# Pooled attention and routed experts on one core: weights in the buffers of k, q and v, row writes held until the last v is in

## The chip, the cores and the metric

The kernel runs on one core of one Trainium2 chip. The metric is device time in microseconds (us) of one execution; where a median is given, it is over several runs. Engines are named as in the profile: PE is TensorE (matrix multiply), PEld its weight loads, DVE is VectorE, ACT is ScalarE, POOL is GpSimd, SP is the sync engine, which here only issues transfers.

## What is computed

Attention with pooled keys and values, and then one of eight experts for each token:

```python
k_p = k.reshape(B, H, Sp, 8, D).mean(axis=3)          # B, H, S, D = 8, 8, 576, 64
v_p = v.reshape(B, H, Sp, 8, D).mean(axis=3)
attn = softmax(q @ k_p.T / sqrt(D))
x = (attn @ v_p).transpose(0, 2, 1, 3).reshape(4608, 512)
for e in range(8):                                     # domain_id: the expert of each token
    mask = domain_id == e
    h = maximum(x[mask] @ w1[e], 0.0)                  # w1: (8, 512, 1024)
    out[mask] = h @ w2[e]                              # w2: (8, 1024, 512)
```

All inputs but domain_id are float32 in HBM; the kernel converts to float16 on the way in.

## The kernel before

**Stages.** Two batch entries are a *pair*; there are four pairs. For each pair, k, q and v (1152 KB each in float16) are loaded whole, one transfer each (load_pair, L107), on GpSimd's queue, which converts. k is pooled by matmuls and turned (kp_units, L416), q is turned (qt_units, L483), v is pooled and turned (vp_units, L449: nine units of matmuls evacuated in three operations at L467, then two folds evacuated at L479; all five evacuations on ScalarE). sc_unit (L499) makes scores and takes their exponential on ScalarE. av_unit (L512) multiplies by v, divides by the sum on VectorE (L530, L532) and leaves three chunks of 128 rows of x in an x_sb tile; after every third chunk SP writes that tile to x_lin in HBM (L541). There are twelve such writes, of 384 KB, three for each pair, and four x_sb tiles.

**Routing.** While attention runs, the kernel works out for each expert the list of its rows in x_lin (perm_units with two GpSimd operations a pair at L370, perm_mm, perm_finish) and of its output rows (orig_finish). An expert has room for 640 rows, five blocks of 128. gather (L583) brings one block from x_lin by an indirect transfer; turn_units (L590) turns blocks for use as the moving operand; l1_units (L623) multiply by w1 and apply the maximum, alternating between ScalarE (L638) and VectorE (L640); l2_units (L644) multiply by w2, evacuate y and scatter each block to the output by an indirect transfer of GpSimd (L659). The first 384 rows of experts 0 and 1 are filled from pairs 0 to 2 alone, so that they can start early: their gathers read only the first part of x_lin and need the first nine row writes.

**Order of the work.** The order is written out by hand. Every engine executes its instructions in program order. In attention, units are put into a plan with a due number (16 for each pair) and sorted by it (L678 to L743): loads, kp, vp, qt, av units, the routing, gathers and the first experts' units each have a due number, and nothing checks it against time. After that, lists of units are run one after the other (L753 to L784). pace (L606) makes GpSimd copy one element of the hidden tile before a gather, so that the gather isn't issued before a given L1 unit is done. An instruction with an unmet wait holds up what follows on its engine; this is true for GpSimd, which issues all loads, gathers and scatters, and for SP, which issues the row writes.

**Buffers.** k, q and v have two tiles of 9216 bytes per partition each. Weights (8192 bytes per partition, w1 and w2 of an expert) have four tiles of their own, tag "w", for experts 0, 1, 5 and 6; the other experts use tiles of k, q and v (W_AT, L559). PSUM tiles are big (two), wide (one) and small (two); rot2 takes big, big, wide in turn for scores, av and L1, and rot1 small, small, wide for L2, each by a counter that runs through the whole kernel.

**Rows of w1.** w1 is loaded so that partition p holds rows 4p to 4p+3, one stretch of 16 KB in HBM (L573). av_unit therefore writes the columns of x in a permuted order (L532). w2 is loaded with partition p holding rows 128k+p (L575).

## Time and profile before

| | us |
|---|---|
| median of 14 runs (261.87 to 265.96) | 264.09 |
| the profiled execution, its own time | 262.69 |
| its span | 261.0 |
| PE busy | 228.7 (88%) |
| DVE busy | 121.0 (46%) |
| POOL busy | 115.5 (44%) |
| ACT busy | 94.2 (36%) |
| software queue of DMA (loads, gathers, scatters) | 79.8% of 16 engines' span |
| hardware queue of DMA (row writes) | 5.0% of 16 engines' span |

The page divides the span into 40 slices of about 6.5 us and gives the busy share of each engine in tenths, the clock granted to TensorE (PEclk, tenths of full speed) and the mean busy share of the 16 DMA engines. In a timeline, a line is a run of equal instructions: start, time, engine, line of the kernel, operation, output and input tile; a bracket at its end gives the engine's idle time before it and what released it. A busy DMA engine or TensorE says where the work is, and the brackets say which wait ended last.

### The profile page before, as it was taken

To read this page: it belongs to the slowest core of one execution; us is meant where nothing else is said; L and a number is where in the kernel's file an instruction comes from. 1 tells how busy PE (TensorE), PEld (TensorE's weight loads), DVE (VectorE), ACT (ScalarE), POOL (GpSimd) and SP (SyncE) were. 2 spreads that over 40 slices of the span, in tenths; PEclk is the share of its full clock that TensorE was granted. 3 is DMA by queue.
4 is the path that set the end of the run, shared out by engine and by line. 5 is a ranking of instruction groups with operands and counts; after the bars stand their busy time and mean duration, and the time that the engine had idled before them with its cause. 6 is when DMAs were issued, how large, how long until landed. Compare 5 with 4: busy or idle time off the path is not lost.

```text
span 261.0 us, 5042 instructions
## 1 busy us (share of the span) xinstructions
PE 228.7 (88%) x2048; PEld 147.3 (56%) x2048; DVE 121.0 (46%) x275; ACT 94.2 (36%) x158; POOL 115.5 (44%) x157
## 2 busy tenths in 40 slices
PE   0788889999788679997966999999999999999991
PEld 0566566676466456555833655755745755756640
DVE  7356698786568444244421333333333332343320
ACT  1046767779367724232310321311311312302210
POOL 8001521300000670177870777676766676654043
PEclk9997999999989757999997999999999999999998
DMA  6999999999998299987899798989979978952022
GB/s 109 205 224 212 219 217 234 244 242 243 244 239 256 65 173 260 238 221 130 244 151 252 130 203 161 221 210 181 228 228 158 225 207 181 219 218 100 3 96 100
DMA packets 18298, 50.20 MB, mean 192 GB/s; under 512 B 2332, under 2 KB 10590, under 8 KB 15840
## 3 DMA queue, kind: packets, MB, share of 16 engines
q0 software_dynamic: 16464, 45.10, 79.8%
q1 hardware_dynamic: 1808, 4.76, 5.0%
q8 instruction: 16, 0.26, 0.4%
q14 instruction: 10, 0.08, 0.1%
HBM read 67.15 MB, written 15.20 MB: 315 GB/s over the span
## 4 chain that ended last, share of the span: by engine, by line
PE 54%; DMA 22%; issue 10%; POOL 6%; ACT 3%; DVE 2%; POOLq 1%
PE big L634 16%; PE small L650 13%; DMA q<-in_q_dram 12%; PE wide L634 7%; DMA v<-in_v_dram 7%; PE wide L650 6%; DMA xg<-x_lin,xrow 3%; POOL out_dram L659 3%; PE turn L598 3%; PE small L464 2%; PE big L506 2%; ACT at L509 1%; PE big L526 1%; PE wide L526 1%; PE small L492 1%
## 5 line engine op out<-in xcount | busy, mean ns | idle before, releaser
L584 POOL DMA_INDIRECT xg<-x_lin,xrow x40 | 41.6, 1040 | 50.1 <-DMA x_lin<-x_sb 36.3
L659 POOL DMA_INDIRECT out_dram<-y,tok x40 | 40.2, 1006 | 51.4 <-DVE y L655 27.8
L650 PEld LDWEIGHTS <-hT 128*128 128x128 f16 x272 | 26.3, 99 | 27.6 <-issue 1.7
L509 ACT ACTIVATE at<-big 72x576 f16<-72x576 f32 x45 | 28.7, 645 | 12.8 <-PE big L506 11.9
L634 PEld LDWEIGHTS <-w 128*128 128x128 f16 x256 | 25.3, 100 | 14.0 <-issue 4.9
L634 PE MATMUL big<-xT,w 128*128 128x320 f16 (+2 forms) x176 | 28.8, 311 | 1.4 <-DVE xT L599 1.4
L640 DVE TENSOR_SCALAR hT<-big 128x640 f16<-128x640 f32 (+1 forms) x21 | 15.3, 729 | 27.3 <-PE big L634 17.6
L657 ACT ACTIVATE y<-small 128x512 f32<-128x512 f32 x14 | 8.4, 597 | 49.8 <-PE small L650 38.2
L599 DVE COPY xT<-turn 128x1024 f16<-128x1024 f16 (+1 forms) x24 | 14.3, 597 | 23.1 <-PE turn L598 21.6
L638 ACT ACTIVATE hT<-big 128x640 f16<-128x640 f32 (+1 forms) x21 | 13.2, 628 | 25.8 <-PE big L634 23.9
L655 DVE COPY y<-small 128x512 f32<-128x512 f32 x13 | 9.0, 691 | 22.1 <-PE small L650 20.1
L650 PE MATMUL small<-w,hT 128*128 128x512 f16 x72 | 18.5, 403 | 0.0
L598 PE MATMUL turn<-ident,xg 128*128 128x128 f16 x160 | 14.1, 228 | 4.8 <-DMA xg<-x_lin,xrow 4.4
L526 PEld LDWEIGHTS <-at 72*128 72x128 f16 (+1 forms) x320 | 14.5, 108 | 6.5 <-issue 3.1
L598 PEld LDWEIGHTS <-xg 128*128 128x128 f16 x160 | 11.3, 102 | 11.2 <-DMA xg<-x_lin,xrow 4.6
L506 PE MATMUL big<-qT,kpT 64*72 64x288 f16 x90 | 14.9, 329 | 2.8 <-DVE qT L496 1.0
L634 PEld LDWEIGHTS <-k 128*128 128x128 f16 x128 | 12.5, 98 | 5.2
L634 PE MATMUL wide<-xT,w 128*128 128x320 f16 (+2 forms) x80 | 13.8, 306 | 1.4 <-DVE y L655 1.4
L532 DVE TENSOR_TENSOR x_sb<-big,rcp 128x512 f16<-128x512 f32 x21 | 14.5, 691 | 0.7
L492 PE MATMUL small<-ident,q 128*128 128x128 f16 x144 | 11.7, 231 | 3.4 <-DMA q<-in_q_dram 1.7
L640 DVE TENSOR_SCALAR hT<-wide 128x640 f16<-128x640 f32 (+1 forms) x11 | 7.9, 715 | 13.8 <-PE wide L634 11.8
L509 ACT ACTIVATE at<-wide 72x576 f16<-72x576 f32 x19 | 12.3, 646 | 5.5 <-PE wide L506 5.3
(155 smaller groups left out, 358.6 us busy)
## 6 DMA issues: line engine op xcount, KB each, us to landing
w<-in_moe_w_dram POOLq DMA_DIRECT2D x8, 1024.0 KB
k<-in_k_dram POOLq DMA_DIRECT2D x4, 1152.0 KB
v<-in_v_dram POOLq DMA_DIRECT2D x4, 1152.0 KB
x_lin<-x_sb SPq DMA_DIRECT2D x12, 384.0 KB, 10.7
q<-in_q_dram POOLq DMA_DIRECT2D x3, 1152.0 KB
k<-in_moe_w_dram POOLq DMA_DIRECT2D x3, 1024.0 KB
v<-in_moe_w_dram POOLq DMA_DIRECT2D x3, 1024.0 KB
q<-in_moe_w_dram POOLq DMA_DIRECT2D x2, 1024.0 KB
```

Source lines behind the costliest of these rows:

```text
L492: nc.tensor.transpose(p[:, j, :], qq[:, 128 * (j0 + j):128 * (j0 + j) + 128], ident[:])
L506: nc.tensor.matmul(p[0:72, par, 0:288], s["kpT"][64 * par:64 * par + 64, bh, :], s["qT"][64 * par:64 * par + 64, :, 8 * bh:8 * bh + 8], st ...
L509: nc.scalar.activation(at[0:72, bh % 8, :].rearrange("p (a c) -> p a c", a=2), p[0:72, :, 0:288], AFT.Exp, scale=1.0 / 64.0)
L526: nc.tensor.matmul(pv[r0:r0 + z - a, h, 0:65], s["at", bt][0:72, h, a:z], s["vp"][0:72, 8 * bt + h, :], start=True, stop=True, skip_group_ ...
L532: nc.vector.tensor_tensor(out=x_sb.rearrange("p (b h a) -> p b h a", b=4, h=H), in0=pv[:, :, 0:64].rearrange("p h (a b) -> p b h a", b=4), ...
L584: i = nc.gpsimd.indirect_dma_start(out=xg[e % 2][:, j, :], out_offset=None, in_=x_lin[0:rows, :], in_offset=bass.IndirectOffsetOnAxis(ap=x ...
L598: nc.tensor.transpose(p[:, j - a, kk, :], xg[e % 2][:, j, 128 * kk:128 * kk + 128], ident[:])
L599: nc.vector.tensor_copy(xts[e][:, :, 128 * a:128 * z].rearrange("p k (j c) -> p j k c", c=128), p[:, 0:z - a])
L634: nc.tensor.matmul(p[:, a, 0:m], w1[:, kk, 128 * fi:128 * fi + 128], xT[:, kk, s0 + m * a:s0 + m * a + m], start=(kk == 0), stop=(kk == 3))
L640: nc.vector.tensor_scalar(out=dst, in0=p[:, 0:nh, 0:m], scalar1=0.0, scalar2=None, op0=ALU.max)
L650: nc.tensor.matmul(p, hT[:, fi, 128 * j:128 * j + 128], w2[:, fi, :], start=(fi == 0), stop=(fi == 7))
L659: i = nc.gpsimd.indirect_dma_start(out=out, out_offset=bass.IndirectOffsetOnAxis(ap=orig[0][:, bl:bl + 1], axis=0), in_=y[:], in_offset=No ...
```

## The change

Six things are changed together.

- The "w" tiles go. All weights are in tiles of k, q and v: expert e has (k, q), (v, k) or (q, v) for e mod 3 = 0, 1, 2. The loads of w1 and w2 of expert 0 are both put at due number 24.0 to 24.2, right behind the load of the last v; they take the tiles of pair 2's k and q, and wait on GpSimd's queue until these have been read.
- Nine x_sb tiles instead of four. The row writes of pairs 0 and 1 are not issued when their rows are done, but all together by x_rows, at due number 40.0. Ahead of them SP issues a small transfer ("gate") that reads an element row of the last v, and so waits until that v is in. The row writes of pairs 2 and 3 are issued where they were, behind it in SP's order.
- w1 is loaded with partition p holding rows 128k+p, four stretches of 4 KB in HBM, and av_unit writes the columns of x in their natural order.
- The five evacuations of the last pair's v are on VectorE.
- The PSUM tile of an L1 or L2 unit is chosen by its place in its expert, not by a running counter (two and one instead of rot2 and rot1).
- In the written order: the last pair's av units are due a little earlier; token steps (orig_finish) are spread over 44 to 62; w2 of expert 2 is loaded behind all gathers of expert 2; w1 and w2 of expert 3 are loaded behind the third and the fourth late L2 unit instead of the first and the third; the steps that count overflowing rows are moved from expert 1 and expert 0 to experts 2 and 3, and the count is read after expert 4 instead of 3.

The diff, without the overflow path and the count's first lines:

```diff
--- before.py
+++ after.py
@@ -68,26 +68,22 @@
     def wide():
         return ps.tile([128, 8, 128], F32, tag="wide", bufs=1, name="wide")
 
-    turns = {"pre": ("big", "big", "wide"), "out": ("small", "small", "wide")}
-    count_ = {"pre": 0, "out": 0}
-
-    def rot(kind):
-        i = count_[kind]
-        count_[kind] = i + 1
-        tag = turns[kind][i % 3]
-        return {"big": big, "wide": wide, "small": small}[tag]()
-
-    def rot2():
-
-        t = rot("pre")
-        ap = t[:]
-        return ap if ap.shape[2] == 512 else ap.rearrange("p (a b) c -> p a (b c)", a=2)
-
-    def rot1():
-
-        t = rot("out")
-        ap = t[:]
-        return ap if len(ap.shape) == 2 else ap.rearrange("p a b -> p (a b)")[:, 0:512]
+    n2 = [0]
+
+    def two(i=None):
+
+        if i is None:
+            i = n2[0]
+            n2[0] = i + 1
+        if i % 3 < 2:
+            return big()[:]
+        return wide()[:].rearrange("p (a b) c -> p a (b c)", a=2)
+
+    def one(i):
+
+        if i % 3 != 2:
+            return small()[:]
+        return wide()[:].rearrange("p a b -> p (a b)")[:, 0:512]
 
     def small():
         return ps.tile([128, 512], F32, tag="small", bufs=2, name="small")
@@ -104,6 +100,7 @@
             return lambda *a, **kw: self.units.append(lambda: getattr(nc.vector, name)(*a, **kw))
 
     x_lin = dram.tile([XROWS, HD], F16, name="x_lin")
+    gate = dram.tile([1, D], F16, name="gate")
     def load_pair(t_ap, pr, tag, cuts=(0, 72)):
         t = wp.tile([128, 72, D], F16, tag=tag, bufs=2, name=tag)
         src = t_ap[2 * pr:2 * pr + 2].rearrange("b h (g t) d -> (b h g) t d", g=8)
@@ -464,9 +461,12 @@
                     nc.tensor.matmul(pv[:, i, :], vv[:, o:o + 128], ident[:],
                                      start=(t == 0), stop=(t == 3), skip_group_check=True)
                 if i == 3 or w == 8:
-                    nc.scalar.activation(
-                        vT[:].rearrange("p b (w g) -> p w b g", g=8)[:, w - i:w + 1],
-                        pv[:, 0:i + 1].rearrange("p w (b g) -> p w b g", g=8), AFT.Copy, scale=0.125)
+                    dst = vT[:].rearrange("p b (w g) -> p w b g", g=8)[:, w - i:w + 1]
+                    src = pv[:, 0:i + 1].rearrange("p w (b g) -> p w b g", g=8)
+                    if pr == NP - 1:
+                        nc.vector.tensor_scalar(out=dst, in0=src, scalar1=0.125, scalar2=None, op0=ALU.mult)
+                    else:
+                        nc.scalar.activation(dst, src, AFT.Copy, scale=0.125)
 
             def fold(b0):
                 if b0 == 0:
@@ -476,7 +476,10 @@
                 for b in range(8):
                     nc.tensor.matmul(pv[0:72, b, :], vT[:, b0 + b, :], FI[:], start=True, stop=True,
                                      skip_group_check=True)
-                nc.scalar.activation(vp[0:72, b0:b0 + 8, 0:64], pv[0:72], AFT.Copy)
+                if pr == NP - 1:
+                    nc.vector.tensor_copy(vp[0:72, b0:b0 + 8, 0:64], pv[0:72])
+                else:
+                    nc.scalar.activation(vp[0:72, b0:b0 + 8, 0:64], pv[0:72], AFT.Copy)
             return ([lambda w=w: unit(w) for w in range(9)]
                     + [lambda: fold(0), lambda: fold(8)])
 
@@ -501,7 +504,7 @@
             if bh % 8 == 0:
                 s["at", bh // 8] = wk.tile([128, H, S], F16, tag="at", bufs=3, name="at")
             at = s["at", bh // 8]
-            p = rot2()
+            p = two()
             for par in range(2):
                 nc.tensor.matmul(p[0:72, par, 0:288], s["kpT"][64 * par:64 * par + 64, bh, :],
                                  s["qT"][64 * par:64 * par + 64, :, 8 * bh:8 * bh + 8],
@@ -512,9 +515,9 @@
         def av_unit(pr, cc):
             s = st[pr]
             if cc % 3 == 0:
-                s["x"] = per.tile([128, 3, HD], F16, tag="x_sb", bufs=4, name="x_sb")
+                s["x"] = per.tile([128, 3, HD], F16, tag="x_sb", bufs=9, name="x_sb")
             x_sb = s["x"][:, cc % 3, :]
-            pv = rot2().rearrange("p a (b c) -> p (a b) c", c=128)
+            pv = two().rearrange("p a (b c) -> p (a b) c", c=128)
             lo, hi = 128 * cc, 128 * cc + 128
             parts = []
             if lo < S:
@@ -528,18 +531,28 @@
                                      skip_group_check=True)
             rcp = wk.tile([128, 8], F32, tag="rcp", bufs=4, name="rcp")
             nc.vector.reciprocal(rcp[:], pv[:, :, 64])
-
-            nc.vector.tensor_tensor(out=x_sb.rearrange("p (b h a) -> p b h a", b=4, h=H),
-                                    in0=pv[:, :, 0:64].rearrange("p h (a b) -> p b h a", b=4),
-                                    in1=rcp[:].unsqueeze(1).unsqueeze(3).to_broadcast([128, 4, 8, 16]),
-                                    op=ALU.mult)
+            nc.vector.tensor_tensor(out=x_sb.rearrange("p (h d) -> p h d", d=D), in0=pv[:, :, 0:64],
+                                    in1=rcp[:].unsqueeze(2).to_broadcast([128, 8, D]), op=ALU.mult)
             if cc % 3 == 2:
-                if pr < EPAIR:
-                    rows, c = x_lin[0:XE, :].rearrange("(p c) d -> p c d", c=EC), NC_ * pr + cc - 2
-                else:
-                    rows, c = x_lin[XE:XROWS, :].rearrange("(p c) d -> p c d", c=LC), NC_ * (pr - EPAIR) + cc - 2
-                i = nc.sync.dma_start(rows[:, c:c + 3, :], s["x"][:])
-                tc.declare_no_dep(i.ins, group="xg", reason="the rows gathered so far are of other pairs")
+                xw[pr, cc] = lambda x=s["x"]: x_write(pr, cc, x)
+                if pr >= 2:
+                    xw.pop((pr, cc))()
+
+        xw = {}
+
+        def x_write(pr, cc, x):
+            if pr < EPAIR:
+                rows, c = x_lin[0:XE, :].rearrange("(p c) d -> p c d", c=EC), NC_ * pr + cc - 2
+            else:
+                rows, c = x_lin[XE:XROWS, :].rearrange("(p c) d -> p c d", c=LC), NC_ * (pr - EPAIR) + cc - 2
+            i = nc.sync.dma_start(rows[:, c:c + 3, :], x[:])
+            tc.declare_no_dep(i.ins, group="xg", reason="the rows gathered so far are of other pairs")
+
+        def x_rows():
+
+            nc.sync.dma_start(gate[:], vt[NP - 1][0:1, 71, 0:64])
+            for key in sorted(xw):
+                xw.pop(key)()
 
         def merge(a, b, start=0.0):
 
@@ -556,23 +569,18 @@
 
         wt = {}
 
-        W_AT = {0: ("w", "w"), 1: ("w", "w"), 2: ("k", "v"), 3: ("q", "k"), 4: ("v", "q"),
-                5: ("w", "w"), 6: ("w", "w"), 7: ("k", "v")}
+        W_AT = [("k", "q"), ("v", "k"), ("q", "v")]
 
         def wload_units(e, which, parts):
             box = {}
 
             def unit(i):
                 if i == 0:
-                    tag = W_AT[e][which]
-                    bufs = 4 if tag == "w" else 2
-                    t = wp.tile([128, 4096] if tag == "w" else [128, 72, D], F16, tag=tag, bufs=bufs, name=tag)
-                    box["t"] = t[:] if tag == "w" else t[:].rearrange("p t d -> p (t d)")[:, 0:4096]
-                    if which == 0:
-                        box["s"] = moe_w1[e].rearrange("(p k) f -> p k f", k=4)
-                    else:
-                        box["s"] = moe_w2[e].rearrange("(k p) f -> p k f", k=8)
-                    box["t"] = box["t"].rearrange("p (k f) -> p k f", k=(4, 8)[which])
+                    tag = W_AT[e % 3][which]
+                    k = (4, 8)[which]
+                    t = wp.tile([128, 72, D], F16, tag=tag, bufs=2, name=tag)
+                    box["t"] = t[:].rearrange("p t d -> p (t d)")[:, 0:4096].rearrange("p (k f) -> p k f", k=k)
+                    box["s"] = (moe_w1, moe_w2)[which][e].rearrange("(k p) f -> p k f", k=k)
                     wt.setdefault(e, []).append(box["t"])
                 n = (4, 8)[which] // parts
                 nc.gpsimd.dma_start(box["t"][:, n * i:n * i + n], box["s"][:, n * i:n * i + n])
@@ -628,7 +636,7 @@
             m = n // nh
 
             def unit(fi):
-                p = rot2()
+                p = two(None if alone else fi)
                 for kk in range(4):
                     for a in range(nh):
                         nc.tensor.matmul(p[:, a, 0:m], w1[:, kk, 128 * fi:128 * fi + 128], xT[:, kk, s0 + m * a:s0 + m * a + m],
@@ -645,7 +653,7 @@
             w2 = wt[e][1]
 
             def unit(j):
-                p = rot1()
+                p = one(j + 1 if s1 - s0 == EARLY else j)
                 for fi in range(8):
                     nc.tensor.matmul(p, hT[:, fi, 128 * j:128 * j + 128], w2[:, fi, :],
                                      start=(fi == 0), stop=(fi == 7))
@@ -694,7 +702,7 @@
                 if pr == NP - 2:
                     at[4:] = [16.1, 17.1, 18.2, 19.3, 20.4]
             else:
-                at = [9.2, 10.7, 12.2, 13.7, 16.1, 17.0, 17.9, 18.8, 19.7]
+                at = [9.2, 10.7, 12.2, 13.7, 16.0, 16.4, 17.0, 17.6, 18.2]
             for j in range(NC_):
                 plan.append((t0 + at[j], len(plan), lambda pr=pr, j=j: av_unit(pr, j)))
             k0, k1 = (2.6, 6.6) if pr < NP - 1 else (0.5, 6.5)
@@ -717,17 +725,17 @@
             put(perm_units(i), k0, k1)
             put([lambda i=i: perm_mm(i)], k1 + 2.3, k1 + 2.3)
         put(perm_finish(), 34.0, 44.0)
-        put(orig_finish(), 49.0, 58.0)
+        put(orig_finish(), 44.0, 62.0)
         for pr in range(2, NP):
             for d, t_ap, tag, kx in ((kt, k, "k", -5.0), (qt_, q, "q", -0.6), (vt, v, "v", 7.0)):
                 put([lambda d=d, t_ap=t_ap, pr=pr, tag=tag: load(d, t_ap, pr, tag)],
                     max(0.1 + 0.1 * len(tag), 16 * pr - 32 + kx), max(0.1, 16 * pr - 32 + kx))
-        put(wload_units(0, 0, 1), 24.0, 24.0)
+        put(wload_units(0, 0, 1) + wload_units(0, 1, 1), 24.0, 24.2)
+        put([x_rows], 40.0, 40.0)
         put([lambda j=j: gather(0, j, XE) for j in range(3)], 54.0, 57.0)
-        put(wload_units(0, 1, 1), 57.1, 57.1)
         put([lambda j=j: gather(1, j, XE) for j in range(3)], 58.0, 61.0)
         put(wload_units(1, 0, 1) + wload_units(1, 1, 1), 61.1, 61.2)
-        put([lambda i=i: run(turn_units_(0, i)) for i in range(2)], 63.6, 64.8)
+        put([lambda i=i: run(turn_units_(0, i)) for i in range(2)], 63.8, 65.0)
         def turn_units_(e, i):
             return [turn_units(e, 0, 3, "small")[i]]
 
@@ -738,7 +746,7 @@
                 e0["hT"] = per.tile([128, 8, EARLY], F16, name="hTe")
                 e0["u"] = l1_units(0, 0, EARLY, e0["hT"], 0, True)
             e0["u"][i]()
-        put([lambda i=i: e0_unit(i) for i in range(8)], 64.7, 69.7)
+        put([lambda i=i: e0_unit(i) for i in range(8)], 64.9, 69.7)
         plan.sort(key=lambda x: x[:2])
         run([x[2] for x in plan])
         att.close()
@@ -755,32 +763,34 @@
         g = [lambda e=e, j=j: gather(e, j) for e in range(2) for j in range(3, NBL)]
         run([u[0], g[0], t[0], u[1], g[1], t[1], u[2], g[2]])
         he = late.tile([128, 8, EARLY], F16, tag="hTl", bufs=1, name="hTe1")
-        u = merge(l1_units(1, 0, EARLY, he, 0), count_a() + [count_mm])
-        run(u[:4] + [pace(he, 0, 0, g[3])] + u[4:])
+        u = l1_units(1, 0, EARLY, he, 0)
+        run(u[:3] + [pace(he, 0, 0, g[3])] + u[3:])
         run(wload_units(2, 0, 1))
         v = l2_units(1, 0, EARLY, he)
         run([v[0]] + turn_units(0, 3, NBL) + [v[1]])
         h0 = hidden()
         g = [lambda j=j: gather(2, j) for j in range(NBL)]
-        u = paced(l1_units(0, EARLY, CAP, h0, 0), h0, 0, g[:3] + wload_units(2, 1, 1), [0, 3, 5, 7])
-        run(merge(u[:7], count_b()) + [v[2]] + turn_units(1, 3, NBL) + u[7:])
+        u = paced(l1_units(0, EARLY, CAP, h0, 0), h0, 0, g[:3], [0, 2, 5])
+        run(u[:7] + [v[2]] + turn_units(1, 3, NBL) + u[7:])
         h1 = hidden()
-        run(paced(l1_units(1, EARLY, CAP, h1, 0), h1, 0, g[3:], [1, 4]))
+        run(paced(l1_units(1, EARLY, CAP, h1, 0), h1, 0, g[3:] + wload_units(2, 1, 1), [0, 3, 6]))
         u = l2_units(0, EARLY, CAP, h0) + l2_units(1, EARLY, CAP, h1)
         t = turn_units(2, 0, NBL)
-        run([u[0], wload_units(3, 0, 1)[0], t[0], u[1], t[1], u[2], wload_units(3, 1, 1)[0], t[2], u[3]])
+        run([u[0], t[0], u[1], t[1], u[2], wload_units(3, 0, 1)[0], t[2], u[3]])
+        run(wload_units(3, 1, 1))
         for e in range(2, E):
             h = hidden()
             u = l1_units(e, 0, CAP, h, 0)
             if e == E - 1:
                 nc.gpsimd.drain()
             g = [lambda j=j: gather(e + 1, j) for j in range(NBL)] if e + 1 < E else []
-            run(paced(u, h, 0, g, [0, 2, 3, 5, 6]))
+            u = paced(u, h, 0, g, [0, 2, 3, 5, 6])
+            run(merge(u, count_a() + [count_mm] if e == 2 else count_b() if e == 3 else []))
             u = l2_units(e, 0, CAP, h)
             t = turn_units(e + 1, 0, NBL) if e + 1 < E else [lambda: None] * 3
             w = wload_units(e + 2, 0, 1) + wload_units(e + 2, 1, 1) if e + 2 < E else [lambda: None] * 2
             run([u[0], w[0], u[1], t[0], u[2], w[1], t[1], u[3], t[2], u[4]])
-            if e == 3:
+            if e == 4:
                 read_count()
 
     main.close()
...
```

## Prediction

> **What bounds the kernel now.** I read the page's slices first, then the chain of waits, then the timelines of TensorE and of GpSimd from 40 to 145 us, then stretches of granted clock, then the DMA view from 40 to 80 us.
>
> ```profile
> PE   0788889999788679997966999999999999999991
> PEclk9997999999989757999997999999999999999998
> DMA  6999999999998299987899798989979978952022
> ```
>
> A slice is 6.5 us. DMA stands at 9 until slice 12 (85 us), and from slice 22 on TensorE is full. From L1 of expert 2 at 144.76 to the end its records leave one gap of 0.33 us, so nothing is to be won there but much can be lost. The time before that is in five places, four of them here (TensorE's timeline; last bracket: idle time and releaser):
>
> ```profile
> 70.77 0.98 PE L492 MATMUL small<-ident,q 128*128 128x128 f16 x8 [1.74 <-DMA q<-in_q_dram]
> 92.03 1.03 PE L598 MATMUL turn<-ident,xg 128*128 128x128 f16 x8
> 96.26 1.44 PE L634 MATMUL big<-xT,w 128*128 128x384 f16 x4 [1.39 <-DVE xT L599]
> 121.30 0.60 PE L634 MATMUL wide<-xT,w 128*128 128x256 f16 x4 [1.38 <-DVE y L655]
> 139.24 0.61 PE L598 MATMUL turn<-ident,xg 128*128 128x128 f16 x4 [4.43 <-DMA xg<-x_lin,xrow]
> 139.64 3.34 PE L650 MATMUL small<-w,hT 128*128 128x512 f16 x8
> ```
>
> The fifth is the clock, in stretches (us; busy time by engine; PEclk, DMA share, GB/s):
>
> ```profile
> 70.70:74.10 3.40, 3.33 (x31) 2.44 (x32) 1.59 (x3) 1.17 (x2) 0.00 (x0) 0.53 1.07 245
> 87.80:101.40 13.60, 10.98 (x98) 7.19 (x95) 6.63 (x17) 4.75 (x9) 7.63 (x8) 0.51 0.85 179
> ```
>
> At half clock the first costs some 1.7 us and the second some 5 us of work. A third stretch follows the 4.43 us wait: eight L2 matmuls took 3.34 us, elsewhere 1.89. On GpSimd's timeline the reader sees who orders the transfers:
>
> ```profile
> 46.04 0.55 POOL L111 DMA_DIRECT2D v<-in_v_dram  x1 [5.92 <-PE big L506]
> 46.58 0.54 POOL L578 DMA_DIRECT2D w<-in_moe_w_dram  x1
> 51.06 1.53 POOL L370 TENSOR_TENSOR vc<-eq,thl 128x360 f16<-128x360 f16 x2 [3.94 <-DVE eq L363]
> 86.48 1.12 POOL L584 DMA_INDIRECT xg<-x_lin,xrow  x1 [33.88 <-DMA x_lin<-x_sb]
> 128.92 0.94 POOL L578 DMA_DIRECT2D v<-in_moe_w_dram  x1
> 130.19 1.05 POOL L584 DMA_INDIRECT xg<-x_lin,xrow  x1
> ```
>
> The last gathers of expert 2 sit behind the 1 MB load of its w2 (128.92); that is the 4.43 us wait.
>
> **What the Trainium skill says.** "DMA: Bandwidth & Descriptors", Queues, rings and completion order: an engine takes turns between queues packet by packet. The trace agrees: from 40.8 to 73.4 us every row write (eight 3072-byte packets per engine, 134 ns) lasts 6.5 us, the time of eight pairs with a 9216-byte packet of q, k, v (699 ns). Same page, SWDGE vs HWDGE vs iDMA: a packet is preferably at most 4096 bytes; in the trace 2.2 to 2.4 pieces of w2 (2 KB read each) pass per row packet. "TensorE: Matmul & The Clock Gate", What's actually happening: an idle window of about 3.4 us halves the clock, until a busy one. The trace agrees: 13.6 us is four such windows.
>
> **The parts, with their cost.** Packet times are from the trace's packet records; w1(e), w2(e) are the weights of expert e.
>
> Rows held. In the DMA view from 40 to 80 us the hardware queue's 868 packets (144 a write) fill 16.4% of the engines: 6.56 us for six writes, 1.09 us each. Some 4.5 of them go before the last q and 5.5 before the last v. So q is in at 70.8 - 4.9 = 65.9 and v at 78.0 - 5.9 = 72.1. TensorE comes to the last q at 69.0, or 0.7 later: w2(0) now waits on GpSimd's queue until pair 2's q is transposed (55.9), and the two vc operations queued behind it (1.53 us), which TensorE needs at 57.45, end near 58.2. The 1.74 us wait and its half-clock window go: the last v's matmuls start near 75.3 instead of 78.0.
>
> Last v on VectorE. Five evacuations leave ScalarE (0.60, 0.60, 0.27, 0.60, 0.59: 2.7 us), where exponentials are late from 83 to 92 us. On VectorE they are 128x512 from PSUM, like L655's copy at 0.69: 3.0 us, beside 12.4 busy of 20. With the first step TensorE could reach the first transposes of gathered rows near 88.5 instead of 92.0.
>
> The price of holding. Those gathers need nine row writes. Now w1(0) and w2(0) stand right behind the last v in GpSimd's queue, and SP's queue is shut until v has landed; behind it wait pair 2's writes too. The engines then have 5.3 (w1) + 5.2 to 6.3 (w2: 200 pieces a us where it runs alone, 98 ns each where it is mixed) + 9 x 1.06 = 20 to 21.1 us from 69.8 on, and the row packets finish last: 90 to 91. Landing takes 1.3 (last row packet 85.1, gather 86.48), so gathers start near 91.8 instead of 86.48, and transposes, 5.2 later, near 97 instead of 92.03. TensorE stands from 88.5 to 97, so what the first two steps won is lost here and the clock is halved again. Then: 3.0 to the first L1 matmul (VectorE between, 4.2 before), 5.9 of L1 and av work at full clock, and 0.7 to 2.1 for half clock until 101.4 or 104.9: L1 of expert 0 ends near 106.7, before 104.8. **+1.9**, bounds -0.5 and +3.9.
>
> w2(0) early: worth nothing, since L2 at 104.78 did not wait for it. w1(1), w2(1) after six gathers (1.35 each): in near 109 and 115, needed near 112.5 and 117.7: nothing.
>
> PSUM turns by position. L1 of expert 0's late part no longer begins on the wide tile that the L2 before it uses: **-1.4**.
>
> w2(2) behind all gathers of expert 2: **-4.4** and the clock window, 1.45 + 0.2: **-1.7**.
>
> What is late next: expert 3's gathers. Call X the start of expert 2's L1. L2 work before it is 8.0 us, so w2(2) is issued at X - 8.2 and ends at X - 1.5 (1.5 us to first packet, 5.2 of data) or X + 0.4 (8.6 after issue, as before). w1(3) moves behind the third scatter, issue near X - 0.2, instead of X - 10.3; w2(3) from X + 0.2 to X + 1.7. In queue order: scatters (0.7 each), w1(3), a scatter, w2(3), two gathers, landing: X + 14.3 to X + 17.3. TensorE wants their transposes at X + 8.7 + 3.5 = X + 12.2. A wait of 2.1 to 5.1; I take **+3.0**, near the low end because the rate seen on a filled queue is 5.2 a load, and **+0.9** for a clock window that may follow (0 to 1.7).
>
> w1 in 2 KB pieces. 624 ns at 8 KB and 98 at 1 KB give 23 + 0.0733 per byte: 692 for four pieces, +11%, 0.55 us an expert; w2's overlap shows that the fixed part can hide, and a gain is excluded because no byte is saved. From expert 4 on some 1.4 us between landing and use cover it: **0**, up to +2.2 for four experts. The row evacuation keeps its 512 elements: 0.69, as in L655's plain copy: 0.
>
> Moved bookkeeping (count steps into experts 2 and 3, the count read one expert later, token steps spread): VectorE operations of 0.2 us where it is 35% busy: 0; without that cover about 0.2 each. The gate's one small DMA and SP's issues (0.32 each) are in the 1.3 allowed above.
>
> Sum: 1.9 - 1.4 - 4.4 - 1.7 + 3.0 + 0.9 = -1.7. The profiled execution took 262.69 (span 261.03 and 1.7 around it), 1.4 under the median of 264.09. Moved by as much, the median becomes **262.4**.
>
> **Rivals.** *The load queue becomes the bound (slower).* At expert 3's transposes the wait is 4.5 with a whole clock window (1.7), gathers start at the late end (+2.9), and w1 costs 0.5 in three experts: 2.9 - 7.5 + 6.2 + 1.5 = +3.1, **267.2**. It decides once wait and clock there pass 5.6 us. For it: w2 loads lasted 6.2 to 8.8 us in the records; against: much of that is the start of an empty queue. *Gains and waits cancel:* **264.1**. *Row writes get through early:* if they pass w1's small pieces fast and gathers start by 87.5, TensorE does not stand, three half-clock windows go (5 us) and the 1.9: -8.6, **255.5**; against it is the equal turn-taking of 40 to 73 us. That the rows are not held at all is excluded: SP issues in order behind a transfer that reads the last v.
>
> **Chances.** Forecast 0.35, early rows 0.10, cancel 0.20, load queue 0.35. A measurement here tells about 0.5% (1.3 us) from no change. Faster 0.45, same 0.20, slower 0.35. The forecast's own range is 259.5 to 262.8; as both signs are likely, the range must reach from part of the early-rows case to past the load-queue case: 257.5 to 268.5.
>
> **What would show it.** Right: no wait for the last q; the first gather issued near 91.8; an idle TensorE of 7 us or more before the first transposes at half clock; no wait at expert 2's transposes; one of about 3 us at expert 3's, none later. Wrong: gathers before 89 (faster than said), or a wait at the transposes of each later expert (w1's pieces), or expert 3's over 4.7 us.

## The result, and the profile after

The changed kernel took 265.65 us (median of 10 runs, 263.35 to 268.44), the kernel before 263.65 (47 runs): ratio **1.0095, 95% interval [1.0061, 1.0129]**. The forecast was 262.4 and faster. The sign is that of the rival "the load queue becomes the bound" (267.2). The same kernel, run again in two later sets of 22 runs each, gave 1.0015 [0.9983, 1.0047] and 1.0008 [0.9979, 1.0036]. So the change is worth nothing or costs up to 1%; no set shows the forecast gain. A set is a group of runs in which a kernel alternates with the kernel before; medians are over all runs of a set, and ratios leave out the runs of a slower state, so a set with many of these (e3: 12 of 22) has a lower ratio than its median suggests. The profiled execution took 265.39 us (span 263.7).

The page's slices of the changed kernel, 6.6 us each, counted from 0:

```profile
PE   0779889979987729999999949999999999999990
PEclk9997999997999556999999997999999999999997
DMA  6999999999999728996949999968989969952032
```

TensorE's hole is now in slices 13 and 14 (86 to 99 us), where the clock is 5: this is where the price of holding is paid. A second hole, a 4, is in slice 23 (152 to 158 us), in the part that was full, and the clock is 7 in the slice behind it. TensorE's timeline of the changed kernel at the places shown of before (last bracket: idle time and releaser):

```profile
58.29 0.48 PE L379 MATMUL small<-vc,op 128*128 128x80 f16 x9 [1.22 <-POOL vc L367]
71.13 0.62 PE L495 MATMUL small<-ident,q 128*128 128x128 f16 x8
96.00 0.61 PE L606 MATMUL turn<-ident,xg 128*128 128x128 f16 x4 [4.21 <-DMA xg<-x_lin,xrow]
97.35 0.61 PE L606 MATMUL turn<-ident,xg 128*128 128x128 f16 x4 [0.74 <-DMA xg<-x_lin,xrow]
99.45 0.61 PE L606 MATMUL turn<-ident,xg 128*128 128x128 f16 x4 [1.05 <-DMA xg<-x_lin,xrow]
122.70 1.04 PE L642 MATMUL big<-xT,k 128*128 128x256 f16 x8
135.12 0.61 PE L606 MATMUL turn<-ident,xg 128*128 128x128 f16 x8
152.86 1.89 PE L658 MATMUL small<-v,hT 128*128 128x512 f16 x8 [0.78 <-DVE y L663]
157.28 0.76 PE L606 MATMUL turn<-ident,xg 128*128 128x128 f16 x8 [2.54 <-DMA xg<-x_lin,xrow]
157.88 3.24 PE L658 MATMUL wide<-v,hT 128*128 128x512 f16 x8
164.30 1.89 PE L658 MATMUL small<-v,hT 128*128 128x512 f16 x8 [0.46 <-ACT y L665]
```

Three waits of before are gone: 1.74 us at the last q (71.13), 1.38 at L1 of expert 0's late part (122.70), 4.43 at expert 2's transposes (135.12). Five have come: 1.22 for vc (two GpSimd operations of the routing, L367), 6.00 for the first gathers in three pieces, 0.78 and 0.46 for PSUM tiles and 2.54 for expert 3's gathers. Eight L2 matmuls at 157.88 take 3.24 us: half clock. The stretches of the changed kernel (as before: us, busy time of PE, PEld, DVE, ACT, POOL, then PEclk, DMA share, GB/s; packets are counted whole where they start, so that a share can pass 1):

```profile
59.20:62.60 3.40, 3.40 (x36) 2.44 (x32) 1.85 (x6) 1.80 (x3) 0.00 (x0) 0.51 1.02 214
86.50:103.50 17.00, 10.04 (x94) 6.54 (x94) 7.68 (x19) 3.92 (x7) 7.93 (x8) 0.50 0.55 172
158.20:161.60 3.40, 3.40 (x15) 1.59 (x13) 1.01 (x2) 0.00 (x0) 0.39 (x1) 0.51 1.12 184
```

The window of the last q has not gone, it is at 59 us now, after the wait for vc; the long one is 17 us instead of 13.6. GpSimd's timeline of the changed kernel:

```profile
45.60 0.55 POOL L108 DMA_DIRECT2D v<-in_v_dram  x1 [5.93 <-PE big L509]
50.51 0.75 POOL L586 DMA_DIRECT2D k<-in_moe_w_dram  x1 [4.36 <-PE big L509]
55.79 0.89 POOL L586 DMA_DIRECT2D q<-in_moe_w_dram  x1 [4.53 <-PE wide L509]
56.70 1.54 POOL L367 TENSOR_TENSOR vc<-eq,thl 128x360 f16<-128x360 f16 x2
93.01 1.13 POOL L592 DMA_INDIRECT xg<-x_lin,xrow  x1 [34.77 <-DMA x_lin<-x_sb]
134.29 0.94 POOL L586 DMA_DIRECT2D v<-in_moe_w_dram  x1
141.60 0.85 POOL L586 DMA_DIRECT2D k<-in_moe_w_dram  x1
143.75 0.96 POOL L586 DMA_DIRECT2D q<-in_moe_w_dram  x1
```

vc is held up by the two loads in front of it, of which w2 waits for q's tile until 55.79. The first gather is issued at 93.01, 6.5 us later than before. In the packet records v ends at 71.7 us, w1 of expert 0 runs from 69.1 to 77.6, its w2 from 74.0 to 90.2, and the nine row writes from 75.8 to 90.6: rows and w2 share the engines and end together, as the prediction's sum had it (90 to 91). Below, w1(e) and w2(e) are expert e's weights, and "L2(0)" is the first L2 matmul of expert 0 (104.78 before, 107.75 after).

### The profile page after: what moved, and what is told of

Its sections match the earlier page's. It is cut to its first block, busy times and chain, and to the rows that moved or that the text cites. A ratio compares the mean times of both kernels' runs of the same rounds, so it can differ in the third digit from the quotient of the medians.

```text
span 263.7 us, 5029 instructions
## 1 busy us (share of the span) xinstructions
PE 228.8 (87%) x2048; PEld 146.3 (55%) x2048; DVE 123.2 (47%) x280; ACT 92.1 (35%) x153; POOL 116.9 (44%) x157
## 4 chain that ended last, share of the span: by engine, by line
PE 56%; DMA 14%; issue 10%; DVE 8%; POOL 6%; ACT 3%; POOLq 1%; DVEq 0%
PE small L658 14%; PE big L642 14%; DMA v<-in_v_dram 7%; DMA xg<-x_lin,xrow 6%; PE wide L642 6%; PE wide L658 4%; POOL out_dram L667 3%; PE turn L606 3%; PE small L461 3%; DVE x_sb L534 3%; PE big L509 2%; PE small L432 2%; ACT at L512 2%; PE big L529 2%; DVE qT L499 2%
## 5 line engine op out<-in xcount | busy, mean ns | idle before, releaser
L648 DVE TENSOR_SCALAR hT<-big 128x640 f16<-128x640 f32 (+1 forms) x24 | 17.4, 724 | 33.2 <-PE big L642 18.0
L663 DVE COPY y<-small 128x512 f32<-128x512 f32 x16 | 11.1, 691 | 28.3 <-PE small L658 26.4
L642 PEld LDWEIGHTS <-v 128*128 128x128 f16 x192 | 18.7, 98 | 9.2 <-issue 1.3
L642 PEld LDWEIGHTS <-k 128*128 128x128 f16 x192 | 18.9, 99 | 8.2 <-issue 0.9
L642 PE MATMUL big<-xT,v 128*128 128x320 f16 (+2 forms) x144 | 22.0, 299 | 0.4 <-issue 0.2
L642 PE MATMUL big<-xT,k 128*128 128x320 f16 (+2 forms) x140 | 21.6, 304 | 0.0
L658 PE MATMUL small<-q,hT 128*128 128x512 f16 x80 | 18.6, 379 | 0.0
L658 PE MATMUL small<-k,hT 128*128 128x512 f16 x80 | 18.4, 379 | 0.0
L658 PE MATMUL small<-v,hT 128*128 128x512 f16 x64 | 14.9, 379 | 1.2 <-DVE y L663 0.8
L642 PEld LDWEIGHTS <-q 128*128 128x128 f16 x128 | 12.4, 98 | 5.2
```

Source lines behind the costliest of these rows:

```text
L642: nc.tensor.matmul(p[:, a, 0:m], w1[:, kk, 128 * fi:128 * fi + 128], xT[:, kk, s0 + m * a:s0 + m * a + m], start=(kk == 0), stop=(kk == 3))
L648: nc.vector.tensor_scalar(out=dst, in0=p[:, 0:nh, 0:m], scalar1=0.0, scalar2=None, op0=ALU.max)
L658: nc.tensor.matmul(p, hT[:, fi, 128 * j:128 * j + 128], w2[:, fi, :], start=(fi == 0), stop=(fi == 7))
```

## The experiments

The theory: the change gains what was forecast (three waits), and loses it through the order of transfers alone, since w2(0) goes ahead of the rows and the weights of experts 2 and 3 are issued late. The rival: the engines are full until 160 us, and whatever the order, what is won in one place is waited for in the next. Sets with the changed kernel itself (i0 and j0, "the repeats" below) were added when a near copy, f3, came out 1.2% below it. The expectations of the e and f runs were laid from the first ratio, 1.0095; their results are read against the repeats, 1.0015 and 1.0008.

| kernel | median (runs) | ratio to before, interval |
|---|---|---|
| changed | 265.65 (10) | 1.0095 [1.0061, 1.0129] |
| changed, i0 and j0 | 263.01, 262.98 (22 each) | 1.0015 [0.9983, 1.0047], 1.0008 [0.9979, 1.0036] |
| e1 rows at once | 259.81 (20) | 0.9894 [0.9871, 0.9917] |
| e3 w2(0) behind six gathers | 262.90 (22) | 0.9948 [0.9917, 0.9979] |
| j1 w2(0) behind three gathers | 257.64 (6) | 0.9873 [0.9803, 0.9942] |
| e2 w2(2) and expert 3 earlier | 263.54 (22) | 1.0030 [1.0007, 1.0053] |
| j2 w1(2) earlier too | 261.40 (22) | 0.9985 [0.9956, 1.0015] |
| i1 count late | 262.89 (22) | 1.0004 [0.9971, 1.0037] |
| e4 w1 in 16 KB | 262.65 (14) | 1.0003 [0.9969, 1.0037] |
| f2 vc first | 261.69 (22) | 0.9990 [0.9966, 1.0014] |
| f3 last v on ScalarE | 261.10 (14) | 0.9974 [0.9932, 1.0016] |
| f4 = e1 + f2 + e4 | 261.30 (22) | 0.9928 [0.9893, 0.9962] |
| **i2 held, loads reordered** | **254.40 (7)** | **0.9718 [0.9660, 0.9776]** |
| i3 at once, loads reordered | 256.90 (6) | 0.9820 [0.9754, 0.9886] |
| f1 before, w2(2) behind | 260.17 (22) | 0.9900 [0.9866, 0.9935] |
| j3 before, loads reordered | 259.48 (20) | 0.9888 [0.9856, 0.9919] |

**The changed kernel again (i0, j0).**

> The changed kernel once more, unedited, on the chip of this group, because f3, which differs from it in five evacuations only, was 1.2% below the ratio first measured for it. If that ratio (1.0095) was a matter of where free-running half-clock windows fell in that set of runs, this one lies at 0.998 to 1.004; if the changed kernel is really slower, 1.006 to 1.012.

> The changed kernel a third time, unedited. The two ratios so far are 1.0095 and 1.0015, with intervals that don't meet. If the change costs some 0.5%, this lies at 1.003 to 1.009; if it costs nothing and the first set of runs stood high by itself, at 0.998 to 1.003; if the first set is right, at 1.007 or more.

Both came out in the lower band. Their profiled executions took 262.04 and 261.84 us, *less* than the 262.69 of before, and lie 1.0 and 1.1 under the medians of their sets. They differ from the first one in three places: L2(0) at 107.40 and 107.23; L1 of expert 1's late part in 3.6 us instead of 4.8 (no record says why it was slow); and full clock after expert 3's wait. Expert 3's wait of i0:

```profile
151.35 1.89 PE L658 MATMUL small<-v,hT 128*128 128x512 f16 x8 [0.78 <-DVE y L663]
155.68 0.76 PE L606 MATMUL turn<-ident,xg 128*128 128x128 f16 x8 [2.44 <-DMA xg<-x_lin,xrow]
```

The waits are those of the first profile, and yet no half clock follows. Stretches of one clock window's length, of the changed kernel, first profile:

```profile
154.80:158.20 3.40, 0.92 (x10) 0.66 (x11) 0.12 (x1) 0.58 (x1) 0.76 (x2) 1.00 1.10 314
```

and of i0:

```profile
151.40:154.80 3.40, 1.83 (x8) 0.63 (x7) 0.00 (x0) 0.60 (x1) 1.85 (x2) 1.00 1.20 260
154.80:158.20 3.40, 2.52 (x20) 1.45 (x21) 0.69 (x1) 0.00 (x0) 1.01 (x1) 1.00 1.07 270
```

In the first the wait fell into one window (0.92 us busy of 3.40), and the next was at half clock; in i0 it was split over two (1.83 and 2.52), and neither was followed by one. So the same wait cost 1.7 us more (1.35 in the eight L2 matmuls, 0.37 in the transposes behind them) or nothing.

**What holding the rows costs (e1, e3, j1).** e1 writes each three chunks when they are done, without the gate:

```diff
-                if pr >= 2:
-                    xw.pop((pr, cc))()
+                xw.pop((pr, cc))()
...
-        put([x_rows], 40.0, 40.0)
```

> The changed kernel, but every row write is issued when its rows are done; nothing waits for the last v. Queue theory (expert 0's gathers start late because nine row writes share the engines with w1 and w2 of expert 0 after the last v): the last v lands some 6 us later, near 77 to 78, but the first gathers are issued near 86 to 88 instead of 93.0, the first transposes start near 92 instead of 96.0, and L2 of expert 0 near 105 instead of 107.8. What comes at expert 3 stays, so the time falls by 1.5 to 3 us against the changed kernel: a ratio of 0.998 to 1.004 to the kernel before. Rival (holding the rows pays, and the loss is elsewhere): TensorE waits for the last q and v again and the time rises by 1 to 4 us: 1.013 to 1.025.

e3 loads w2(0) behind the six early gathers (due 61.05), j1 behind the first three:

```diff
-        put(wload_units(0, 0, 1) + wload_units(0, 1, 1), 24.0, 24.2)
+        put(wload_units(0, 0, 1), 24.0, 24.0)
+        put(wload_units(0, 1, 1), 57.1, 57.1)
```

> The changed kernel, but w2 of expert 0 is loaded behind the first six gathers instead of behind the last v. Queue theory: the row writes share the engines with w1 of expert 0 alone, so the first gathers are issued near 87 to 88 instead of 93.0 and TensorE hardly waits before the first transposes; the two vc operations no longer stand behind that load, so TensorE's wait of 1.2 us at 58.3 and the half-clock window after it go. 3 to 5 us less than the changed kernel, a ratio of 0.991 to 0.999. Rival (what is won at the gathers is lost when L2 of expert 0 waits for its w2): L2 of expert 0 starts no earlier than 107 and the time is within 1 us of the changed kernel, 1.006 to 1.013.

> The changed kernel with w2 of expert 0 loaded between the two triples of early gathers, and nothing else. Theory: the row writes come in before it, the first gathers start near 86.2, L2 of expert 0 at 104 to 105 instead of 107.5; the 2.5 us wait at expert 3's transposes stays: about 3 us, 0.987 to 0.993 (0.010 to 0.013 below the changed kernel of this group). Rival, what is won before 110 us is lost at expert 3's transposes, since the transfers ahead of them end when they did: 0.996 to 1.003, with a wait of over 4 us there.

e1 is 3.2 us under the repeats, more than expected: in this order holding is a loss. The path is not quite the expected one: the first gather is issued at 89.66 (86 to 88 was expected), L2(0) starts at 105.23, and no half-clock window follows expert 3's wait. The last q costs no wait here either, because TensorE, late from the wait for vc, comes to it only at 71.77. e3 shows what holds the gathers up, and the limit. Its gathers start at 86.18, but w2(0) is then late, so that L2(0) starts at 105.98, 1.2 to 1.4 us before the repeats (ratio 0.9948, in the theory's range); TensorE's timeline of e3:

```profile
89.66 0.61 PE L606 MATMUL turn<-ident,xg 128*128 128x128 f16 x4
105.98 3.57 PE L658 MATMUL small<-q,hTe 128*128 128x512 f16 x8 [4.39 <-DMA q<-in_moe_w_dram]
```

j1 finds the place between. GpSimd's timeline of j1:

```profile
86.15 1.11 POOL L592 DMA_INDIRECT xg<-x_lin,xrow  x1 [34.15 <-DVE rcp L533]
89.91 0.97 POOL L586 DMA_DIRECT2D q<-in_moe_w_dram  x1
```

and TensorE's of j1:

```profile
90.61 1.04 PE L606 MATMUL turn<-ident,xg 128*128 128x128 f16 x8
93.59 0.61 PE L606 MATMUL turn<-ident,xg 128*128 128x128 f16 x4 [1.50 <-DMA xg<-x_lin,xrow]
151.07 0.76 PE L606 MATMUL turn<-ident,xg 128*128 128x128 f16 x8 [1.90 <-DMA xg<-x_lin,xrow]
```

The rows have only the end of w1(0) beside them and are in at 84.8; the first gather goes 6.9 us earlier than in the changed kernel, the first wait is 1.50 instead of 6.00, L2(0) starts at 102.41, and expert 3's wait does not grow. It is 0.0135 below the repeat of its set by the ratios, 3.5 us (5.3 by the medians, of six runs), as expected or a little more. The rival's "lost again at expert 3" is refuted. One move of one load is worth more than the whole change.

**The loads of experts 2 and 3 (e2, j2, f1).** e2 puts w2(2) right behind w1(2) and expert 3's loads to the places of before; j2 puts w1(2) ahead of expert 1's L1 and w2(2) where w1(2) was, with expert 3's loads as in e2 (j2's edit, without that part):

```diff
+        run(wload_units(2, 0, 1))
         he = late.tile([128, 8, EARLY], F16, tag="hTl", bufs=1, name="hTe1")
...
-        run(wload_units(2, 0, 1))
+        run(wload_units(2, 1, 1))
         v = l2_units(1, 0, EARLY, he)
...
-        run(paced(l1_units(1, EARLY, CAP, h1, 0), h1, 0, g[3:] + wload_units(2, 1, 1), [0, 3, 6]))
+        run(paced(l1_units(1, EARLY, CAP, h1, 0), h1, 0, g[3:], [0, 3]))
```

> The changed kernel, but w2 of expert 2 is loaded right behind its w1, and w1 and w2 of expert 3 behind the first and third late L2 unit, as in the kernel before. Queue theory (three loads in a row stand ahead of expert 3's gathers): the waits before expert 3's transposes (0.8 and 2.5 us) and the half-clock window behind them go, at most 1.5 us of waiting comes at expert 2's transposes; 4 to 6 us less than the changed kernel, a ratio of 0.987 to 0.995. Rival (the rate of the transfers as such is the limit, with w1's smaller pieces in it, and order only moves the wait): a wait of 2 us or more stands before expert 2's or expert 4's transposes, and the time is within 1.5 us of the changed kernel: 1.004 to 1.015.

> The changed kernel with only the loads of experts 2 and 3 put forward (w1 of expert 2 ahead of expert 1's L1, its w2 where w1 was, expert 3's at the places of before). Theory: waits at the transposes of experts 2 and 3 are under 1 us but for the 0.78 us of the held PSUM tile, L2 of expert 0 stays near 107.5: 2.5 to 4 us, 0.987 to 0.994 (0.009 to 0.014 below the changed kernel of this group). Rival, as when w2 of expert 2 alone was put forward (e2), the wait moves to expert 2's transposes: within 0.004 of the changed kernel, with over 2 us of wait there.

e2: no wait for expert 3's gathers, but one at expert 2's:

```profile
136.56 0.95 PE L606 MATMUL turn<-ident,xg 128*128 128x128 f16 x8 [3.34 <-DMA xg<-x_lin,xrow]
```

Here the rival is right: the wait moves (3.34 us where the theory allowed 1.5), and nothing is won (1.0030). In j2 what is left of it is

```profile
135.23 0.80 PE L606 MATMUL turn<-ident,xg 128*128 128x128 f16 x8 [1.61 <-DMA xg<-x_lin,xrow]
```

and none at expert 3's. j2 is 1.6 us under the repeats by the medians and 0.0023 by the ratios, with overlapping intervals: the time is the rival's, though the wait is under the rival's 2 us. f1 is the kernel before with only the change's place of w2(2), behind all gathers of expert 2:

```diff
-        u = paced(..., g[:3] + wload_units(2, 1, 1), [0, 3, 5, 7])
+        u = paced(..., g[:3], [0, 2, 5])
...
-        run(paced(l1_units(1, EARLY, CAP, h1, 0), h1, 0, g[3:], [1, 4]))
+        run(paced(l1_units(1, EARLY, CAP, h1, 0), h1, 0, g[3:] + wload_units(2, 1, 1), [0, 3, 6]))
```

> The kernel before with one part of the change alone: w2 of expert 2 is loaded behind all five gathers of expert 2. Queue theory (three loads come too close together, whoever is first): the wait of 4.4 us before expert 2's transposes goes and its half-clock window with it, and a wait of 1.5 to 3.5 us comes at expert 3's transposes instead, though expert 3's w1 is still loaded early; 2 to 4 us less, a ratio of 0.985 to 0.993. Rival (the reordering is a clean gain and the loss lies in the other parts): no wait over 1 us at expert 3's transposes, 5 to 6 us less, 0.975 to 0.981.

As the theory had it, 2.5 us: the 4.43 us wait and its window go, and at expert 3's gathers a wait comes, with expert 3's loads still where they were:

```profile
155.31 1.04 PE L598 MATMUL turn<-ident,xg 128*128 128x128 f16 x8 [3.48 <-DMA xg<-x_lin,xrow]
```

So the wait there comes from w2(2)'s place and not only from the later loads of expert 3.

**Small parts (i1, e4, f2, f3, f4).** i1: in the changed kernel the count's matmul takes one of two small PSUM tiles in expert 2's L1 and holds it until it is read in expert 3's; with one tile left, L2 waits 0.78 and 0.46 us for y to be evacuated. i1 moves that matmul to expert 3's L1.

```diff
-            run(merge(u, count_a() + [count_mm] if e == 2 else count_b() if e == 3 else []))
+            if e == 3:
+                count_mm()
+            run(merge(u, count_a() if e == 2 else count_b() if e == 3 else []))
```

> The changed kernel with the count's matmul moved out of expert 2's L1 to just before expert 3's, where its result is read, so that no small PSUM tile is held through expert 2's L2. If the held tile causes the 0.78 us wait before expert 3's transposes and the 0.46 us wait later in the same L2, both go and the kernel is 0.5 to 1.2 us (0.002 to 0.005) below the changed kernel of this group. Rival, the gathers' wait grows by what is taken away (it ends last there): the 0.46 us alone goes, at most 0.002 below.

Both waits are gone, and TensorE waits longer for the gathers:

```profile
155.25 1.03 PE L606 MATMUL turn<-ident,xg 128*128 128x128 f16 x8 [3.34 <-DMA xg<-x_lin,xrow]
```

Medians 0.1 us apart: the rival is right, the held tile hid under a wait that ends later. e4 loads w1 with partition p holding rows 4p+k again, in 8 KB packets, with x in the permuted column order:

```diff
-                    box["s"] = (moe_w1, moe_w2)[which][e].rearrange("(k p) f -> p k f", k=k)
+                    box["s"] = moe_w1[e].rearrange("(p k) f -> p k f", k=k) if which == 0 else moe_w2[e].rearrange("(k p) f -> p k f", k=k)
```

> The changed kernel, but w1 is loaded by rows 4p+k in one stretch of 16 KB for each partition, and the columns of x are permuted again. Queue theory: the loads of w1 take 0 to 0.5 us less each, which matters only before the first gathers and before expert 3's transposes: 0 to 1 us less than the changed kernel, a ratio of 1.005 to 1.010. Rival (w1's small pieces are what made it slower): 2.5 us less or more, 1.000 or under.

No difference to the repeats; beside the first ratio it would have looked like the rival's 2.5 us. f2 puts expert 0's loads behind vc on GpSimd's queue:

```diff
-        put(wload_units(0, 0, 1) + wload_units(0, 1, 1), 24.0, 24.2)
+        put(wload_units(0, 0, 1) + wload_units(0, 1, 1), 29.2, 29.4)
```

> The changed kernel, but the loads of expert 0 are put behind the two vc operations in GpSimd's order. TensorE's wait of 1.22 us at 58.3 and the half-clock window after it (59.2 to 62.6) should go, so that TensorE comes to the last q some 2.5 us earlier. Queue theory: the first gathers are still issued near 92 to 93, so that TensorE only waits longer before the first transposes: within 1 us of the changed kernel, 1.006 to 1.012. Rival (lost time of TensorE in attention is on the path): 2 us less or more, 1.002 or under.

The wait for vc and its clock window go, the last q starts at 67.98 and the last v at 73.78; but the first transposes stay where they were:

```profile
95.41 0.61 PE L606 MATMUL turn<-ident,xg 128*128 128x128 f16 x4 [6.69 <-DMA xg<-x_lin,xrow]
```

What was won is waited away. Against the repeats the ratio is 0.002 lower (1.3 us by the medians) and the intervals overlap: the theory's "within 1 us" holds, though 0.9990 lies in the band that the rival had drawn from the first ratio. f3 evacuates the last v on ScalarE, with the lines of before at L467 and L479.

> The changed kernel, but the last v is evacuated by ScalarE again. Queue theory: TensorE comes to the first transposes up to 1 us later or earlier (its wait before the first fold, 1.08 now, was 0.81 before), but it waits there for the gathers anyway: within 1 us of the changed kernel, 1.006 to 1.013. Rival (ScalarE's exponentials decide): 1.5 us more or over, 1.015.

Neither theory: the first fold waits 0.81 us instead of 1.08, all else stays. VectorE is no gain; whether it is a small loss isn't told apart. f4 joins e1, f2 and e4.

> The changed kernel with three parts undone or mended: row writes at once, vc ahead of the loads of expert 0, w1 in 16 KB pieces. Rows at once alone gave 0.989. With the rows not held, the path to the first gathers is the work of TensorE and ScalarE in attention, so the 2.5 us of the vc wait and its clock window now count, and w1's pieces some 0.5 to 1: a ratio of 0.978 to 0.986. Rival (the parts do not add, the queue of loads sets the end): within 1 us of rows at once, 0.986 to 0.992.

The parts don't add, as the rival had it: f4 is not below e1. With the rows written early and vc no longer late, TensorE waits for the last q again (1.78 us), so that vc first is worth nothing.

**All loads reordered (i2, i3, j3).** i2 is j1 + j2 + i1. i3 is i2 with e1's edit. j3 is the kernel before with j2's places for w1(2) and w2(2).

> Rows still held, but the load queue reordered at every place where a wait was found: expert 0's w2 behind the first three gathers, expert 2's w1 ahead of expert 1's L1 and its w2 where w1 was, expert 3's at the places of before, the count's matmul late. Theory (the slowdown is the order of transfers): no wait over 1 us at the transposes of experts 2 and 3, first L2 of expert 0 within 1 us of before's 104.8, 0.978 to 0.988. Rival (the engines are full up to 160 us, so that a load moved forward only delays gathers elsewhere): 0.992 to 1.003, with a wait of 2 us or more at one of these places.

> The same order of loads with the rows written at once, no gate. Theory: both gains come together, L2 of expert 0 starts at 103 to 105, no wait over 1 us at the transposes of experts 2 and 3, 0.975 to 0.984, below every kernel so far. Rival, as for the last: 0.987 to 0.995, about what rows at once gave alone (0.989).

> The kernel before, with expert 2's w1 and w2 put forward in the same way (expert 3's stand where they stood). If the rest of the change (rows held, PSUM turn by position, last v on VectorE) is worth its 1.4 us of PSUM turn and 1.7 us of the half-clock window at the last q in this order, this kernel is at 0.980 to 0.986, 3 us above the held and reordered one (0.972). Rival, the whole gain is the order of loads: 0.970 to 0.975, no different from it.

i2 beats both kernels: 8.1 us under before, 8.6 under the changed kernel by the medians, more than expected. It also beats the sum of its parts: by the ratios it is 0.030 under the repeat of its set, j1, j2 and i1 alone 0.014, 0.002 and 0.001. Alone, j1 leaves a wait of 1.90 us at expert 3's gathers, and j2 one of 1.61 at expert 2's besides those for the first gathers. TensorE's timeline of i2:

```profile
69.67 0.62 PE L495 MATMUL small<-ident,q 128*128 128x128 f16 x8
92.93 1.03 PE L606 MATMUL turn<-ident,xg 128*128 128x128 f16 x8
124.59 0.40 PE L606 MATMUL turn<-ident,xg 128*128 128x128 f16 x4 [1.53 <-DMA xg<-x_lin,xrow]
131.92 0.75 PE L606 MATMUL turn<-ident,xg 128*128 128x128 f16 x8
150.50 0.61 PE L606 MATMUL turn<-ident,xg 128*128 128x128 f16 x8
```

No wait for the first gathers nor at expert 2's and 3's; the one of 1.53 us is at expert 1's late rows. The same weights and rows are moved, so "the engines are full whatever the order" is refuted. Nor is the clock the cause: i2's profile has a mean clock of 0.938, before's 0.950. The same order in the kernel before (j3) is 5.1 us slower, where 3 were expected, with these waits among others:

```profile
70.82 0.62 PE L492 MATMUL small<-ident,q 128*128 128x128 f16 x8 [1.78 <-DMA q<-in_q_dram]
110.62 1.48 PE L634 MATMUL big<-xT,w 128*128 128x384 f16 x8 [1.68 <-DMA w<-in_moe_w_dram]
120.73 0.60 PE L634 MATMUL wide<-xT,w 128*128 128x256 f16 x4 [0.78 <-DVE y L655]
```

None of the three is in i2; the first goes by the held rows, the third by the PSUM turn, and for the second no run tells which part does it. So the rest of the change does pay once the loads stand right. Holding pays too then, against the expectation of i3: it has the wait for q back,

```profile
70.69 0.67 PE L495 MATMUL small<-ident,q 128*128 128x128 f16 x8 [1.74 <-DMA q<-in_q_dram]
```

and is 2.5 us slower than i2 (intervals overlap; the times, 253.82 to 256.47 and 255.66 to 258.59, hardly do). In the order as changed, it was the other way round (e1).

## Why the prediction was wrong

**The sum, by its terms.** Differences to before of the starts in the timelines: to L2(0); from there to the first L2 matmul of expert 2 (153.45 before); from there to the last L2 (251.60 before).

| | forecast | first profile | i0 | j0 |
|---|---|---|---|---|
| first gathers, to L2(0) | +1.9 | +2.97 | +2.62 | +2.45 |
| PSUM turn, w2(2), its window | -7.5 | -6.24 | -7.39 | -7.39 |
| expert 3's transposes, window | +3.9 | +5.55 | +3.73 | +3.60 |
| sum | -1.7 | +2.28 | -1.04 | -1.34 |

**What failed** is the size of two terms, the price of holding and expert 3's, a piece at the end that no term has, and the step from one execution to the median. The mechanism of the two terms held.

*Price of holding* (+1.9): measured +2.97, +2.62 and +2.45. The row packets ended at 90.7 as summed, but the first gather followed 2.3 us later and not 1.3 (1.4 and 1.7 in the repeats). The transposes then began at 96.00, not 97, but in three pieces. The prediction's own terms put the end of expert 0's L1 at 106.6 to 108.0, by how long half clock lasts, to 101.4 or 104.9, and it took the early end; half clock lasted to 103.7 and L2(0) began at 107.75.

*Expert 3's transposes* (+3.0 of wait, +0.9 of clock): the waits there are 0.78, 2.54 and 0.46, together 3.78, and 3.68 and 3.56 in the repeats. The forecast had only the gathers; the two short ones come from the count's PSUM tile, a part of the moved bookkeeping that was put at nothing for a reason of VectorE alone. i1 shows that the first of them costs no time, since the wait for the gathers grows by as much; what the second costs is too small for the sets to tell. The 0.9 was the mean of nothing and a whole window, and the profiles show both ends: 1.7 in the first, none in the repeats.

*Late gains* (-7.5): -7.39 in the repeats, as said. In the first profile 1.2 us more lie in L1 of expert 1's late part, with no releaser shown.

*The end*: from the last L2 to the end of the span it is 9.43 us in before and 9.82 to 9.89 in the three profiles of the changed kernel: 0.4 us that no term has. f1 and j3, built on the kernel before, have 9.43. Which part of the change does it is open.

For the first profile this adds up: 1.1 + 1.6 + 1.3 + 0.4 = 4.4 us above the forecast of -1.7 makes +2.7, the measured difference of the spans (263.73 and 261.03). That execution lay 0.3 us under the median of its set and not 1.4, which takes 1.1 off again: 3.3 us, the distance from 262.4 to 265.65.

*The signs.* Most of those named for "right" were seen, and none of those for "wrong", and yet the time went the other way: they told of the places and not of the sizes. The one that failed is the idle TensorE of 7 us or more before the first transposes: it was 6.00, 2.62 and 5.06.

*The rest.* w1's pieces at 0: right (e4). Rows held, last q: the wait went as forecast, and v started at 76.93, not 75.3. "TensorE needs vc at 57.45, which ends near 58.2" left the clock out: the 1.22 us wait brought a half-clock window of its own, so that the window at the last q came back at 59 us. Last v: TensorE came to the first transposes at 91.8 (96.00 - 4.21), not 88.5; nothing followed from either, as the gathers were later still (f2). "2.2 to 2.4 pieces of w2 pass per row packet", read in the kernel before, does not carry over: from 77.7 to 86.6 us of the changed kernel it was 689 pieces to 674 row packets, about one to one. The end of the rows, summed from all the bytes, didn't hang on it.

**The last step**, "moved by as much, the median becomes 262.4", failed too: it took one execution for the middle of its kind. Before's profile lay 1.4 us under the median of its 14 runs; the changed kernel's lay 0.3, 1.0 and 1.1 under those of their sets. The repeats' profiles are 0.65 and 0.85 us shorter than before's, the sign that was forecast, and yet their medians are 0.5 longer. So of the 2.2 us by which the repeats miss, 0.8 to 1.1 lie in the terms and the end, and 1.2 to 1.4 between single executions and medians.

**Open**: what these 1.2 to 1.4 us are. The clock is a candidate, not shown. Averaged over all runs of a set it is 0.950 to 0.953 for the kernel before and 0.937, 0.938 and 0.941 for the changed one, and among runs of the kernel before the span grows by 0.8 to 1.2 us for each 0.01 of clock; that would make 1.0 to 1.5. Against it: i0's profiled execution has a clock of 0.935, below the mean of its set, and is still shorter than before's (0.950). It spent 6.8 us at half clock behind the wait for vc, j0 3.4, and L2(0) came only 0.17 us later, as TensorE waited less for the gathers. And j1 and i2, the fastest of their sets, spend 23.9 us on end at half clock (from 75.0 and 76.5 us on), the kernel before 13.7. In these runs half clock cost time where TensorE's work was what the rest waited for, so a mean over the run does not price it.

Open too is why the first set stands 2.6 us above the repeats. Its mean clock (0.937) is theirs, so it isn't the clock; the kernel before stood 1.0 to 1.2 us higher in that set as well.

**The rival** "load queue" had the sign, and three of its terms in part: gathers at the late end (+2.97 against +2.9), a whole window at expert 3's (first profile only), but no 4.5 us wait there, and nothing for w1. "Gains and waits cancel" is what the repeats show. The load queue was more a matter of order than of its rate: i2 moves the same bytes in 8.6 us less.

## What to carry to other kernels

When transfers of a queue are put in another order, work out for each consumer what stands in front of it: here the whole change moved the time by at most 1%, and the place of one 1 MB load beside it by 1.3% (j1). Whether to hold small writes back is no question by itself: in i2 against i3 it paid, where only the next needed load went beside the rows, and in the changed kernel against e1 it lost, where one more load did. And count a stall with the clock that may follow it, as a range and not as its mean, and set a forecast of 0.6% against the scatter of single executions.

## What the runs showed of the hardware

Over the 18 traces of this case I cut the time from the first half-clock window to 240 us into windows of 3.413 us that begin at the recorded changes of clock, and took TensorE's busy share in each. At full clock: under 0.50 busy, half clock followed in 10 of 14; from 0.50 to 0.75, in 21 of 53; from 0.75 to 0.80, in 2 of 34; above, in none of 792. At half clock: under 0.80 busy, half clock stayed in all 41; above, full clock came in 51 of 92. The first two counts depend on where the windows are laid (0.3 us earlier they are 9 of 9 and 24 of 55); that over 0.80 none fell and under 0.80 none rose stays. So half a window idle can be enough, and getting out needs a nearly full one. "TensorE: Matmul & The Clock Gate" of the Trainium skill, section What's actually happening, tells of an idle window of about 3.4 us; here a window that was still busy for 1.88 us of 3.40 did it (from 55.8 us on in the first profile, 1.22 us of wait and some shorter gaps).

Held row writes, of 3072-byte packets, followed each other every 1.0 us once w1 was in (121 ns a packet, j1, 76.4 to 82.2 us), and every 1.8 us with w2 beside them (changed kernel, six writes, 75.8 to 86.6 us). Each of before's took 6.5 us among the loads of q, k and v. So the nine held writes took 10.7 us in j1 and 14.8 in the changed kernel, by which load shared the engines with them.
